# Fourth pair's loads behind a one-hot DMA, second pair's assignment in the PV bank, fourth pair's transposes later: the opening of a routed-attention and FFN kernel

## Chip, core and metric

The kernel runs on one core of one Trainium2 chip. The metric is the device time of one launch in microseconds (us). Before the change 12 runs gave a median of 343.56 us, from 342.28 to 346.72.

## What is computed

Attention with 4 batches, 8 heads, 768 positions and head size 64, in which a query sees only the keys that fall into its own one of 16 clusters, and then a gated feed-forward layer over all 3072 tokens:

```python
q_assign = argmax(einsum('bhsd,hcd->bhsc', q_n, c_n))      # k_assign likewise
scores   = where(q_assign == k_assign, q @ k.T / sqrt(64), -1e9)
attn     = softmax(scores) @ v                              # [4, 8, 768, 64]
x        = attn as [3072, 512]; xn = x / rms(x) * rms_g
out      = (silu(xn @ w_gate) * (xn @ w_val)) @ w_out       # 512 -> 1536 -> 512
```

## The kernel before, in words

**Work units.** Two heads of one batch are a pair; there are 16, numbered 0 to 15, so "the fourth pair" is pair 3. A head of a batch is a slot; pair p owns slots 2p and 2p+1. Each pair is prepared, then its two slots are scored, exponentiated and multiplied with v; the FFN of a batch follows while later slots are worked on.

**Preparing a pair** (`prep_parts`, L178 to L275) makes thirteen steps: four transpose groups T0 to T3 (L195: three 128x128 fp32 transposes on TensorE, then one copy of the 128x384 result out of PSUM, L199 or L201); CAST (L218) puts the transposed q and k as bf16 into `aug`; SP (L231) is the cluster product, eight small matmuls; TR, MX, CMP, SCL and BACK (L238 to L259) are the chain on VectorE that makes a one-hot row of it: transpose, maximum, compare, scale, transpose back into `ohT`; PLACE (L272) sends `ohT` by four DMAs of 24 KB into the lower rows of `aug`, one for each of two heads `a` and two sides (q or k); CASTV (L223) casts v on GpSimd. The mask is in the product itself: 64 rows of q or k and 16 rows of one-hot.

**The main loop** (L540 to L554) has 9 steps for a slot. At every third step `score_chunk` (L281) makes four matmuls into a PSUM tile of three banks (`scw`, two such tiles) and one exponential over 1536 columns on ScalarE (L302). I call these groups G0, G1, G2 (slot 0), G3 to G5 (slot 1) and so on, and their exponentials E0, E1 and so on. At steps 2 to 7 of a slot `pv_group` (L306) multiplies the slot before with v, in the one bank `acc`; at step 8 `pv_norm` (L316) divides by the sum on VectorE (L322, L323), and the next slot's product with v needs that bank back. From step 96 on the scores come in single chunks and each step also carries one piece of the FFN: gp, vp (L401) or dp (L434).

**What orders the work.** Nothing is scheduled: the order is written out by hand, and each engine takes its instructions in program order. `at(step, ...)` (L466) hangs a preparation step behind a loop step. All loads of q, k and v are on the queue of SyncE (SP), with three buffers for each of `q_in`, `k_in` and `v_in`: a fourth load waits until the first buffer's readers are done. Before the loop the PSUM tiles come from six banks `f`; from the loop on every transpose group and every cluster product takes the single bank `t` of `ps_t` (`t_tile`, L172), so each must wait until VectorE has read the one before it. Dummy matmuls (`keep_warm`, L125) fill TensorE before the loop.

**The opening** (L470 to L505). Pair 0 is prepared at once, pairs 1 and 2 are transposed, and so is group T0 of pair 3, into a tile that `keep_warm` has used (`late[3, 0]`, L484, L190). Then the loop starts with G0, which needs pair 0's one-hot rows. Pair 1's assignment hangs on steps 0 to 3, pair 2's on steps 4 to 18, pair 3's T1 to T3 on steps 10 to 15.

**The last batch.** Its rows are normalised after the loop by the plan of L513 to L521: `sumsq`, `inv`, `norm` (L367), and then a transposing DMA into `xnT` (L370), which the FFN of that half waits for.

Of the kernel before, what the change touches and what calls it, by code (L numbers as in the profile page):

```python
# [8 lines left out]
F32 = mybir.dt.float32  # L9
# [10 lines left out]
def kernel(  # L20
# [12 lines left out]
    nc = tc.nc  # L33
# [3 lines left out]
    P = 128  # L37
# [41 lines left out]
    def load_part(pi, kind, eng=nc.sync):  # L79
        b, hp = divmod(pi, NP)  # L80
        src, nm = ((q, "q_in"), (k, "k_in"), (v, "v_in"))[kind]
        src = src[b, 2 * hp:2 * hp + 2]
        tl = ld.tile([P, 2, ST * D], F32, name=nm, tag=nm)
        eng.dma_start(out=tl, in_=src.rearrange("h (p t) d -> p h (t d)", p=P))
        loads[pi, kind] = tl
# [5 lines left out]
    c_in = const.tile([P, D + 1], F32, name="c_in")  # L91
    nc.vector.memset(c_in[:, D:D + 1], 1e-15)
    nc.scalar.dma_start(out=c_in[:, 0:D], in_=centroids.rearrange("h c d -> (h c) d"))
    for pi in range(4):
        load_pair(pi, (0, 1))
    load_part(0, 2)
    g_b = const.tile([P, DM], F32, name="g_b")


# [78 lines left out]
    def prep_parts(pi):  # L178
        st = pi % NSET
        qk32 = [None]  # L180
        state = {}

        def t_group(g):
            a, side = divmod(g, 2)
            if qk32[0] is None:
                qk32[0] = prep.tile([P, 4, HS], F32, name="qk32", tag="qk32", bufs=3)
            if pi == 2 and g > 1:
                tp = ((ps_t, ps_pv)[g - 2]).tile([P, HS], F32, name="tp", tag=("t", "acc")[g - 2])
            elif (pi, g) in late:
                tp = late[pi, g][:, 0:HS]  # L190
            else:
                tp = t_tile("tp")
            src = loads[pi, side]
            for i in range(TH):
                nc.tensor.transpose(tp[:, i * P:(i + 1) * P], src[:, a, i * P:(i + 1) * P], ident_f)  # L195
            dst = qk32[0][:, g, :]
            on_dve = (g in (0, 3) if pi == 0 else g == 3 if pi == 2 else pi < 7 or g % 2)
            if on_dve:
                nc.vector.tensor_copy(dst, tp)  # L199
            else:  # L200
                nc.scalar.copy(dst, tp)  # L201
            state[g] = tp

        def casts():
            if pi == 0:
                for g in (0, 2, 1, 3):
                    a, side = divmod(g, 2)
                    for par in range(2):
                        dst = aug[0][a][0:D, side, par * HS:(par + 1) * HS]
                        src = state[g][par * D:(par + 1) * D, :]  # L210
                        if g == 3:
                            nc.vector.tensor_copy(dst, src)
                        else:
                            nc.scalar.copy(dst, src)
                return
            for a in range(2):
                for par in range(2):
                    nc.gpsimd.tensor_copy(aug[st][a][0:D, :, par * HS:(par + 1) * HS],  # L218
                                          qk32[0][par * D:(par + 1) * D, 2 * a:2 * a + 2, :])

        def casts_v():
            v_in = loads[pi, 2]
            nc.gpsimd.tensor_copy(vbf[st][:, :, :, 0:D],  # L223
                                  v_in[:, :, :].rearrange("p a (t d) -> p a t d", d=D))

        def assign():
            h0 = 2 * (pi % NP)
            sp = t_tile("sp")
            for j in range(4):
                side, a = divmod(j, 2)  # L230
                nc.tensor.matmul(sp[32 * j:32 * j + 32, :], lhsT=cbd[:, h0 + a, :, :].rearrange("p c r -> p (c r)"),  # L231
                                 rhs=qk32[0][:, 2 * a + side, :], start=True, stop=True,
                                 tile_position=(0, 32 * j))
            state["sp"] = sp

        def oh_tr():
            tr = prep.tile([P, HS], F32, name="tr", tag="tr")
            nc.vector.transpose(tr, state["sp"])  # L238
            state["tr"] = tr[:, :].rearrange("p (n c r) -> p n r c", c=NC, r=2)

        def oh_max():
            mx = small.tile([P, TH * 4, 2], F32, name="mx", tag="mx")
            nc.vector.tensor_reduce(mx, state["tr"], axis=AX, op=ALU.max)
            state["mx"] = mx

        def oh_cmp():
            oh = prep.tile([P, HS], BF16, name="oh", tag="oh")
            nc.vector.tensor_tensor(oh[:, :].rearrange("p (n c r) -> p n r c", c=NC, r=2), state["tr"],  # L248
                                    state["mx"].unsqueeze(3).to_broadcast([P, TH * 4, 2, NC]), op=ALU.is_ge)
            state["oh"] = oh  # L250

        def oh_scale():
            oh = state["oh"]
            nc.vector.tensor_scalar(oh[0:64, :], oh[0:64, :], scalar1=1.0, scalar2=MASK,
                                    op0=ALU.subtract, op1=ALU.mult)

        def oh_back():
            ohT = prep.tile([P, HS], BF16, name="ohT", tag="ohT")
            nc.vector.transpose(ohT, state["oh"])  # L259
            state["ohT"] = ohT  # L260

        def place():
            ohT = state["ohT"]
            for a in range(2):
                for side in range(2):
                    r = 32 * (2 * side + a)
                    eng = nc.sync
                    if pi == 0:
                        eng = nc.gpsimd if side else nc.scalar
                    elif pi == 1 and (a or side):  # L270
                        eng = nc.gpsimd
                    eng.dma_start(out=aug[st][a][D:KA, side, :].rearrange("c (r n) -> c r n", r=2),  # L272
                                  in_=ohT[r:r + 2 * NC, :])

        return [lambda: t_group(0), lambda: t_group(1), lambda: t_group(2), lambda: t_group(3), casts, assign, oh_tr, oh_max, oh_cmp, oh_scale, oh_back, place, casts_v]  # L275


# [188 lines left out]
    def at(step, fn):  # L466
        extra.setdefault(step, []).append(fn)
# [13 lines left out]
        p0[i]()  # L481
    for i in (T0, T1, T2, T3):
        p1[i]()
    late[3, 0] = keep_warm(3)  # L484
    for i in (T0, T2, T1, T3):
        p2[i]()
    p3[T0]()
    load_part(1, 2, nc.scalar)
    p1[CAST]()
    keep_warm(4)  # L490
    first.close()
    late["wide"] = wide.enter_context(tc.tile_pool(name="ps_wide", bufs=2, space=PSUM,
                                                 reuse_waits="tile"))
    at(2, p0[CASTV])
    for i, step in ((SP, 0), (TR, 0), (MX, 1), (CMP, 2), (SCL, 2), (BACK, 3), (PLACE, 3), (CASTV, 5)):
        at(step, p1[i])
    for i, step in ((T1, 10), (T2, 12), (T3, 15), (SP, 19), (TR, 20), (MX, 21), (CMP, 22), (SCL, 23), (BACK, 24),
                    (PLACE, 24), (CAST, 24), (CASTV, 28)):
        at(step, p3[i])
    for i, step in ((SP, 4), (TR, 5), (MX, 10), (CMP, 12), (SCL, 15), (BACK, 18), (PLACE, 18), (CAST, 6), (CASTV, 14)):  # L500
        at(step, p2[i])
    for pi in range(2, 4):
        at(3, lambda pi=pi: load_part(pi, 2))
# [5 lines left out]
    for b in range(B):  # L509
        sumsq, inv, norm, turn = rms_parts(b)  # L510
        if b == 0:
            plan = [(sumsq, (-9, -7, -4), (0, 1, 2), 0), (sumsq, (8, 8, 8), (0, 1, 2), 1), (inv, (8,), (0,), 2),
                    (norm, (12, 17, 18), (0, 1, 2)), (turn, (17, 20, 22), (0, 1, 2)),  # L513
                    (sumsq, (27, 29, 30), (3, 4, 5)), (inv, (30,), (1,)), (norm, (32, 33, 34), (3, 4, 5))]
        else:
            early = (8, 8, 9, 9, 10, 11, 12) if b == B - 1 else (9, 9, 10, 11, 12, 13, 15)
            plan = [(sumsq, early[:3], (0, 1, 2)), (inv, early[3:4], (0,)), (norm, early[4:], (0, 1, 2)),
                    (sumsq, (19, 19, 25), (3, 4, 5)), (inv, (26,), (1,)), (norm, (27, 28, 29), (3, 4, 5))]
        for fn, steps, items, *more in plan:
            for step, it in zip(steps, items):  # L520
                at(H * NCH * (b + 1) + step, lambda fn=fn, it=it, more=more: fn(it, *more))  # L521
    at(30, lambda: load_pair(6))
    for pi in range(4, B * NP):
        base = 2 * NCH * (pi - 2) + {7: 14, 8: 10, 9: 4}.get(pi, 0)
        steps = (-11, -8, -5, -2, 0, 0, 2, 3, 4, 5, 6, 7, 10)
        if pi == 6:
            steps = (-11, -8, -5, -2, 0, 0, 2, 3, 4, 4, 5, 6, 7)
        elif pi > 6:
            steps = (-8, -6, -4, -2, 0, 0, 2, 3, 4, 5, 6, 6, 10)
        for fn, step in zip(prep_parts(pi), steps):  # L530
            at(base + step, fn)
        if pi < B * NP - 3:
            at({6: 100, 7: 118}.get(pi, base + 12), lambda pi=pi: load_pair(pi + 3))
# [62 lines left out]
```

The softmax here doesn't subtract the row's maximum and nothing guards it: scores larger than these inputs give would overflow.

## Time and profile before

| what | value |
|---|---|
| median of 12 runs | 343.56 us |
| the profiled execution: time | 344.23 us |
| the profiled execution: span from first to last instruction | 342.4 us |
| mean granted TensorE clock | 1.000 |
| TensorE busy | 331.6 us, 97% of the span |
| VectorE busy | 222.7 us, 65% |
| ScalarE busy | 225.5 us, 66% |
| GpSimd busy | 89.0 us, 26% |
| DMA, mean over the span | 102 GB/s |

The span is cut by the profile into instructions with start and duration; the time of a run also holds 1.83 us around the span. The shares of busy time hide that the limits change: the opening (until G0 starts at 14.97 us), the loop without the FFN (until about 62 us), the loop with it (until about 267 us) and the FFN alone. The chain of waits is read from the end backwards: each piece is the work that released the next one.

### The profile page before, as it was taken

The numbers are of one execution on the slowest core, as the hardware profiler recorded it, in microseconds if no ns is written. First come the engines' busy times: TensorE is split into PE (matmuls) and PEld (weight loads), VectorE is DVE, ScalarE is ACT, GpSimd is POOL, SyncE is SP. The second block draws the span as 40 slices with busy tenths as digits, with TensorE's granted clock in tenths as the row PEclk, the third lists the DMA queues.
The fourth block names the chain that finished last, engine by engine and source line by source line (L and its number), as shares of the span: only waits on it lengthen the run. The fifth ranks groups of instructions, "written<-read, shape, count | busy, mean of one in ns | idle before, by whom it ended". The sixth has DMA issues, their size and how long they took to land.

```text
span 342.4 us, 7497 instructions
## 1 busy us (share of the span) xinstructions
PE 331.6 (97%) x2922; PEld 203.2 (59%) x2955; DVE 222.7 (65%) x460; ACT 225.5 (66%) x388; POOL 89.0 (26%) x123
## 2 busy tenths in 40 slices
PE   8899999999999999999999999999999999999996
PEld 4556666666666565666656566566666655555553
DVE  4787697698764777866475567774554687655540
ACT  4498999978776687766767677777777353323322
POOL 2577695066431133230111205010000011000000
PEclk9999999999999999999999999999999999999999
DMA  7747999909744125161501003120000022300012
GB/s 232 243 153 227 239 260 257 255 11 176 208 149 134 48 77 154 42 186 39 173 3 42 33 12 79 35 55 33 31 12 24 31 57 55 78 31 31 33 62 92
DMA packets 36771, 34.99 MB, mean 102 GB/s; under 512 B 13520, under 2 KB 33664, under 8 KB 36736
## 3 DMA queue, kind: packets, MB, share of 16 engines
q1 hardware_dynamic: 30240, 29.20, 27.7%
q0 software_dynamic: 5984, 4.84, 9.0%
q10 hardware_dynamic: 512, 0.48, 0.5%
q8 instruction: 23, 0.38, 0.5%
q14 instruction: 12, 0.10, 0.1%
HBM read 28.61 MB, written 6.29 MB: 102 GB/s over the span
## 4 chain that ended last, share of the span: by engine, by line
PE 86%; DVE 6%; ACT 3%; DMA 3%; issue 2%; POOLq 0%; POOL 0%; DVEq 0%; ACTq 0%
PE gp L401 17%; PE vp L401 17%; PE dp L434 17%; PE sc L299 12%; PE acc L313 9%; PE tp L195 5%; PE scw L299 3%; PE sp L231 3%; ACT pT L302 2%; DMA aug<-ohT 1%; PE w_ps L129 1%; DMA xnT<-xn 1%; DVE oh L248 1%; DVE tr L238 1%; DVE qk L199 1%
## 5 line engine op out<-in xcount | busy, mean ns | idle before, releaser
L302 ACT ACTIVATE pT<-sc 128x512 bf16<-128x512 f32 x192 | 113.8, 598 | 45.4 <-PE sc L299 44.9
L410 DVE SCALAR_TENSOR_TENSOR uu<-th,gp 128x384 f32<-128x384 f32 x96 | 53.0, 552 | 66.2 <-ACT th L406 66.1
L401 PE MATMUL gp<-xnT,wg 128*128 128x384 bf16 x384 | 78.1, 325 | 0.2
L401 PE MATMUL vp<-xnT,wv 128*128 128x384 bf16 x384 | 78.1, 325 | 0.2 <-DVE gvT L416 0.2
L406 ACT ACTIVATE th<-gp 128x384 f32<-128x384 f32 x96 | 47.3, 492 | 43.1 <-PE gp L401 40.5
L313 PEld LDWEIGHTS <-pT 128*128 128x128 bf16 x1152 | 57.1, 97 | 29.3 <-DVE x L323 2.6
L299 PE MATMUL sc<-aug 80*128 80x512 bf16 (+1 forms) x256 | 72.9, 326 | 0.0
L434 PE MATMUL dp<-wo,gvT 128*128 128x512 bf16 (+1 forms) x268 | 71.2, 369 | 1.6
L218 POOL CAST aug<-qk 64x768 bf16<-64x768 f32 x60 | 51.9, 866 | 52.6 <-DVE qk L199 34.4
L313 PE MATMUL acc<-vbf,pT 128*128 128x65 bf16 x1152 | 63.2, 194 | 1.4 <-DVE x L323 0.7
L416 DVE TENSOR_TENSOR gvT<-uu,vp 128x384 bf16<-128x384 f32 x96 | 52.6, 548 | 5.9 <-PE vp L401 0.8
L401 PEld LDWEIGHTS <-wg 128*128 128x128 bf16 x384 | 37.2, 97 | 30.4 <-issue 1.0
L401 PEld LDWEIGHTS <-wv 128*128 128x128 bf16 x384 | 37.1, 97 | 18.7 <-issue 0.6
L302 ACT ACTIVATE pT<-scw 128x1536 bf16<-128x1536 f32 x32 | 44.9, 1457 | 5.0 <-PE scw L299 4.5
L299 PEld LDWEIGHTS <-aug 80*128 80x128 bf16 x384 | 33.0, 97 | 18.1 <-issue 7.4
L434 PEld LDWEIGHTS <-gvT 128*128 128x128 bf16 x300 | 29.1, 98 | 24.4
L199 DVE COPY qk<-tp 128x384 f32<-128x384 f32 x40 | 21.8, 552 | 15.3 <-PE tp L195 15.0
L299 PE MATMUL scw<-aug 80*128 80x512 bf16 (+1 forms) x128 | 26.0, 325 | 1.1 <-DMA aug<-ohT 0.9
L358 POOL TENSOR_SCALAR ir<-ss 128x3 f32<-128x3 f32 x7 | 1.7, 237 | 95.2 <-ACT jk L344 83.4
L367 DVE SCALAR_TENSOR_TENSOR xn<-x,ir,g_b 128x512 bf16<-128x512 bf16 x24 | 20.3, 862 | 6.5 <-POOL ir L359 5.4
L223 POOL CAST vbf<-v_in 128x768 bf16<-128x768 f32 x16 | 13.4, 836 | 34.7 <-issue 34.3
L323 DVE TENSOR_TENSOR x<-acc,inv 128x384 bf16<-128x384 f32 x32 | 17.8, 557 | 1.1
(65 smaller groups left out, 210.0 us busy)
## 6 DMA issues: line engine op xcount, KB each, us to landing
q_in<-in_q_dram SPq DMA_DIRECT2D x16, 384.0 KB, 5.1
k_in<-in_k_dram SPq DMA_DIRECT2D x16, 384.0 KB, 5.8
out_dram<-ob SPq DMA_DIRECT2D x23, 256.0 KB, 2.0
v_in<-in_v_dram SPq DMA_DIRECT2D x15, 384.0 KB, 5.5
wg<-in_moe_w_gate_dram POOLq DMA_DIRECT2D x4, 384.0 KB, 10.7
wv<-in_moe_w_val_dram POOLq DMA_DIRECT2D x4, 384.0 KB, 11.3
wo<-in_moe_w_out_dram POOLq DMA_DIRECT2D x4, 384.0 KB, 7.0
aug<-ohT SPq DMA_DIRECT2D x57, 24.0 KB, 1.9
```

The source lines that it names most:

```text
L199: nc.vector.tensor_copy(dst, tp)
L218: nc.gpsimd.tensor_copy(aug[st][a][0:D, :, par * HS:(par + 1) * HS], qk32[0][par * D:(par + 1) * D, 2 * a:2 * a + 2, :])
L299: nc.tensor.matmul(sc[:, o:o + n], lhsT=ag[:, 1, kc * P:(kc + 1) * P], rhs=ag[:, 0, qo:qo + n], start=True, stop=True)
L302: nc.scalar.activation(pts[slot][:, j * CH:(j + nch) * CH], sc[:, :nch * CH], ACT.Exp, scale=scale)
L313: nc.tensor.matmul(acc[:, TORD[g], :], lhsT=pts[slot][:, kc * S + g * P:kc * S + (g + 1) * P], rhs=vb[:, a, TORD[kc], :], start=(kc == 0), ...
L323: nc.vector.tensor_tensor(x_t[b][:, :, h * D:(h + 1) * D], acc[:, :, 0:D], inv.to_broadcast([P, ST, D]), op=ALU.mult)
L367: nc.vector.scalar_tensor_tensor(st["xn"][:, tl, :], x_t[b][:, t, :], st["ir", m][:, tl:tl + 1], g_b, op0=ALU.mult, op1=ALU.mult)
L401: nc.tensor.matmul(pt[:, :HS], lhsT=w[:, dc, fc * P:(fc + 1) * P], rhs=xnT[b, m][:, :, dc, :], start=(dc == 0), stop=(dc == DC - 1))
L406: nc.scalar.activation(th, pt[:, :HS], ACT.Tanh, scale=0.5)
L410: nc.vector.scalar_tensor_tensor(uu, th, 1.0, pt[:, :HS], op0=ALU.add, op1=ALU.mult)
L416: nc.vector.tensor_tensor(gvT[half][:, fc, :], uu, pt[:, :HS], op=ALU.mult)
L434: nc.tensor.matmul(dp, lhsT=gvT[hf][:, f, tl * P:(tl + 1) * P], rhs=wo[:, f, cols], start=(f == 0), stop=(f == FC - 1))
```

## The change

- Loads: before the loop's order is laid down only q and k of pairs 0, 1 and 2 are asked for. q and k of pair 3 and v of pairs 0 and 1 are asked for later in the program, so that on SP's queue they stand behind one of pair 0's four one-hot DMAs, which moves from ScalarE's queue to SP's. v of pair 1 moves from ScalarE's queue to SP's.
- Pair 3's T0 moves from before G0 to step 5; T1, T2 and T3 from steps 10, 12 and 15 to 7, 9 and 11. It now uses bank `t`. One more dummy matmul stands before G0.
- Pair 1's cluster product goes to the bank `acc`; its CMP, SCL, BACK and PLACE move by one or two steps.
- Pair 2's SP to PLACE move from steps 4 to 18 to steps 13 to 19; pair 3's from 19 to 24 to 20 to 25. Pair 4's T0 and T1 stand one step later.
- In the last batch the second and third `norm` stand one step earlier.

```diff
-    for pi in range(4):
+    for pi in range(3):
         load_pair(pi, (0, 1))
-    load_part(0, 2)
...
-            elif (pi, g) in late:
-                tp = late[pi, g][:, 0:HS]
...
-            sp = t_tile("sp")
+            if pi == 1:
+                sp = ps_pv.tile([P, HS], F32, name="sp", tag="acc")
+            else:
+                sp = t_tile("sp")
...
-                    if pi == 0:
+                    if pi == 0 and (side or not a):
                         eng = nc.gpsimd if side else nc.scalar
...
-    late[3, 0] = keep_warm(3)
+    load_pair(3, (0, 1))
+    load_part(0, 2)
+    load_part(1, 2)
+    w_ps = keep_warm(3)
     for i in (T0, T2, T1, T3):
         p2[i]()
-    p3[T0]()
-    load_part(1, 2, nc.scalar)
     p1[CAST]()
-    keep_warm(4)
+    keep_warm(5, w_ps)
...
-    for i, step in ((SP, 0), (TR, 0), (MX, 1), (CMP, 2), (SCL, 2), (BACK, 3), (PLACE, 3), (CASTV, 5)):
+    for i, step in ((T0, 5), (T1, 7), (T2, 9), (T3, 11), (SP, 20), (TR, 21), (MX, 22), (CMP, 23), (SCL, 24), (BACK, 25),
+                    (PLACE, 25), (CAST, 25), (CASTV, 28)):
+        at(step, p3[i])
+    for i, step in ((SP, 0), (TR, 0), (MX, 1), (CMP, 3), (SCL, 4), (BACK, 5), (PLACE, 5), (CASTV, 5)):
         at(step, p1[i])
-    for i, step in ((T1, 10), (T2, 12), (T3, 15), (SP, 19), (TR, 20), (MX, 21), (CMP, 22), (SCL, 23), (BACK, 24),
-                    (PLACE, 24), (CAST, 24), (CASTV, 28)):
-        at(step, p3[i])
-    for i, step in ((SP, 4), (TR, 5), (MX, 10), (CMP, 12), (SCL, 15), (BACK, 18), (PLACE, 18), (CAST, 6), (CASTV, 14)):
+    for i, step in ((SP, 13), (TR, 14), (MX, 15), (CMP, 16), (SCL, 18), (BACK, 19), (PLACE, 19), (CAST, 6), (CASTV, 14)):
         at(step, p2[i])
...
-            early = (8, 8, 9, 9, 10, 11, 12) if b == B - 1 else (9, 9, 10, 11, 12, 13, 15)
+            early = (8, 8, 9, 9, 10, 10, 11) if b == B - 1 else (9, 9, 10, 11, 12, 13, 15)
...
-        if pi == 6:
+        if pi == 4:
+            steps = (-10, -7, -5, -2, 0, 0, 2, 3, 4, 5, 6, 7, 10)
+        elif pi == 6:
```

## The prediction, as put on record before the run

> **What bounds the kernel now.** I read the chain of waits first, because TensorE is 97% busy and a share that high says nothing about where a change can help. G0, E0 and so on are the score groups and exponentials as named above; T3.0 to T3.3 are pair 3's transpose groups.
>
> Chain of waits, in order of time (start us, length us, what):
>
> ```profile
> 11.83 3.09 DMA aug<-ohT
> 14.97 0.82 PE scw L299 x4
> ...
> 34.23 0.85 PE sp L231 x8
> ...
> 57.03 3.92 ACT pT L302 x3
> ...
> 278.65 0.81 PE vp L401 x4
> 280.34 3.74 DMA xnT<-xn
> 284.13 0.82 PE gp L401 x4
> ```
>
> The loop's start hangs on pair 0's one-hot DMA. From there to 30 us VectorE and TensorE take turns in the chain, to 54 us TensorE with the waits for `pv_norm`, then ScalarE, then TensorE. At 284.13 the transposed `xnT` of the last batch ends a wait. So only two places of the change touch the chain: the opening, and the `norm` steps.
>
> The table of stretches (length, then busy PE, PEld, DVE, ACT, POOL, granted clock, DMA share, GB/s) shows how tight the opening is:
>
> ```profile
> 20.00:25.00 5.00, 5.00 (x65) 3.31 (x64) 3.80 (x8) 5.00 (x5) 4.82 (x8) 1.00 0.68 211
> 25.00:30.00 5.00, 4.04 (x58) 2.84 (x54) 4.83 (x10) 4.18 (x4) 4.76 (x6) 1.00 0.77 231
> ```
>
> TensorE is full from 20 to 25, VectorE from 25 to 30: work moved into either stretch is paid there. The timeline (start, length, engine, idle time before) gives the durations:
>
> ```profile
> 11.56 1.31 ACTq L272 DMA_DIRECT2D aug<-ohT  x2
> 11.83 1.29 POOL L272 DMA_DIRECT2D aug<-ohT  x2 [7.20 <-DVE ohT L259]
> ...
> 15.72 0.85 PE L231 MATMUL sp<-qk,cbd 128*32 128x384 f32 x8
> ...
> 16.64 0.58 DVE L238 STREAM_TRANSPOSE tr<-sp 128x384 f32<-128x384 f32 x1 [2.36 <-PE sp L231]
> ...
> 18.76 0.58 DVE L259 STREAM_TRANSPOSE ohT<-oh 128x384 bf16<-128x384 bf16 x1
> ...
> 20.51 0.81 PE L299 MATMUL scw<-aug 80*128 80x512 bf16 x4
> ...
> 24.97 0.56 DVE L323 TENSOR_TENSOR x<-acc,inv 128x384 bf16<-128x384 f32 x1
> ...
> 25.78 0.81 PE L299 MATMUL scw<-aug 80*128 80x512 bf16 x4
> ```
>
> Seen from G0's start s = 14.97, VectorE begins pair 1's chain at s+1.67 and reaches BACK at s+3.79; G4 starts at 20.51, G7 at 25.78 behind the norm of slot 0.
>
> **One-hot of pair 0: -0.7 us.** G0 reads the two DMAs of head 0, which stay on ScalarE and GpSimd and are issued at the same time (11.56, 11.83); only one of head 1 moves to SP. The gain must come from the emptier queue: in the trace q and k of pair 3 and v of pair 0, issued at 6.01, 7.20 and 7.62, land at 12.4, 13.4 and 14.5. Pair 1's four one-hots, with little else in flight, took 2.1 to 2.7 us, median 2.4, against 3.09. So 11.83 + 2.4 = 14.23 for 14.92: G0 at 14.25, gain 0.7. Bounds: nothing, and 11.83 + 2.1 = 13.93, a gain of 1.0. TensorE is not later: T3.0 goes (0.36), one dummy matmul comes (0.21, from 1.03 less 0.17 over about four).
>
> [...]
>
> **The loads, late: hidden.** SP issues its one-hot (0.69) at 11.6, then q3, k3, v0, v1, v2 at about half a microsecond each from 12.3. A load into an empty queue landed 3.5 us (v1 on ScalarE's queue) to 4.1 us (v2 at 20.11) after its issue, and the next ones follow by 1.0 (384 KB at 376 to 399 GB/s): q3 16.1, k3 17.1, v0 18.1, v1 19.2. T3.0 can run at 16.4, its copy not before 18.0 (below); v0's cast of 0.83 ends at 19.0, and the first product with v comes at 20.1. Cover about 1 us each. v3 waits for v0's cast; behind it on SP stand pair 1's one-hot (ready 19.1) and pair 4's loads, needed after 28. Behind the cast on GpSimd stand three one-hots of pair 1 (G6, 24.3) and pair 2's casts. If v0 came over 1 us later, this cover would go and each further microsecond would count fully.
>
> **G0 to G4: +1.5 us against s.** Every T3 group takes bank `t` and must wait for VectorE's copy of the group before. With s = 14.25: the cluster product at s+0.75, TR, MX, CMP and SCL as in the trace from s+1.67, and T3.0's copy (0.56) in BACK's old place, s+3.79 to s+4.35. T3.1 starts at s+4.4, and G3 stands behind it: s+4.75, E3 at s+5.6 (before: 20.28, s+5.31). BACK then fills VectorE until s+4.93, T3.1's copy until s+5.5; T3.2 at s+5.55 (result after 0.52), its copy s+6.1 to s+6.65, T3.3 at s+6.7, and G4 behind it at s+7.06 = 21.3. Before, G4 stood at s+5.54. Net with the one-hot: 21.3 - 20.51 = +0.8.
>
> **G4 to G7: +0.3 us.** Before, pair 2's cluster product (0.79) ran between G1 and G2, where TensorE waited for exponentials; now it stands between G4 and G5, where TensorE is full. From G4's start: 0.65 + two products with v (0.36), cluster product, result at +1.87; then TR, MX, CMP (0.62 each) stand ahead of the norm of slot 0 on VectorE (0.15 + 0.56): done at +4.5 to +4.75, the larger where CMP shares time with GpSimd's casts (0.81 instead of 0.58 at 22.38). Then one product with v (0.19) and pair 3's cluster product (0.79): G7 at +5.5 to +5.75. Before: 25.78 - 20.51 = 5.27. Net at G7: +1.0 to +1.3; I take +1.1.
>
> **G7 to the end of the loop: 0.** The same instructions in the same order, but for pair 4's T0 and T1 one step later: one wait for the norm shortens as another grows. Chain pieces follow each other without a wait on anything at a fixed time (loads and weights are early), so the delay is carried whole. If some wait had slack that the chain doesn't show, up to 0.5 of it could be lost there.
>
> **The last batch: +0.4 us.** VectorE's order here:
>
> ```profile
> 277.38 0.75 DVE L367 SCALAR_TENSOR_TENSOR xn<-x,ir,g_b 128x512 bf16<-128x512 bf16 x1 [1.35 <-POOL ir L359]
> 278.05 0.55 DVE L416 TENSOR_TENSOR gvT<-uu,vp 128x384 bf16<-128x384 f32 x1
> 278.51 1.41 DVE L367 SCALAR_TENSOR_TENSOR xn<-x,ir,g_b 128x512 bf16<-128x512 bf16 x2
> ```
>
> All wait for `ir`, so an earlier place gains nothing: the three norms and the product together still end at 279.92. But the second norm now stands ahead of gvT, which ends at 279.3 instead of 278.60, and vp at 278.65 started just behind it (it reuses the PSUM tile that gvT reads). TensorE slips by 0.70. It had 0.25 to 0.3 in hand before `xnT` at 284.13 (three dp matmuls from 283.19 end at 283.84), so 0.4 remains. Bounds: 0, if the tile is free sooner than I read it, and 0.7. SP now issues this transpose ahead of one output DMA; the output has three buffers and waits harmlessly.
>
> **Sum.** -0.7 + 1.5 + 0.3 + 0.4 = +1.5 us. Against the profiled execution, 344.23 + 1.5 = 345.7; that execution is 0.67 above the median, and against the median it is **345.1 us**, 0.4% slower. The unknowns together: one-hot ±0.3 to 0.7, the shared time with GpSimd ±0.3, the last batch ±0.4: 343.9 to 346.4.
>
> **Rivals.**
> - *The exponentials keep up* (faster): E7 waited 0.82 us and E10 0.56 for scores, both because VectorE was late with a norm. If pair 2's chain, now in one piece, frees VectorE sooner there, and the gaps at G3 and G4 are refilled, the change is -0.7 - 0.82 - 0.56 + 0.4 = -1.7: 341.9. It decides at E7 before 26.6. For it: ScalarE was busy 5.00 of 5 from 20 to 25. Against it: T3.1 behind the copy is an order that no timing removes. 13%.
> - *The delay is absorbed*: the opening's loss meets slack before 62 us and only the last batch pays, or both cancel: 343.6, from 343.1 to 344.0. Against it stands the unbroken chain. 15%.
> - *v0 is late* (slower by more): the loads need 1.5 us each, v0 lands after 19.5, GpSimd stands at its cast with pair 1's one-hots and pair 2's casts behind it, and the product with v starts after 20.7. Price: another 1 to 2 us, 346.6. For it: v0 is now third in a queue that starts at 12.3. 12%.
> - Forecast: 60%.
>
> A difference under 0.5% (1.7 us) is about what a measurement of this kernel can't tell from none. The forecast's own spread puts about 45% of it beyond that: slower 0.12 + 0.60 x 0.45 plus a little for the unexpected, 0.42; faster 0.13; same 0.45. The range takes in most of both outer rivals: 342.5 to 347.0.
>
> **What would show it.** Right: G0 at about 14.2, a wait of TensorE for VectorE's copy before T3.1 and T3.3, G4 near 21.3, G7 near 26.9, and at the end vp starting behind gvT with `xnT` no longer the last to arrive. Wrong: E3 to E6 without a gap, G7 before 26, TensorE waiting for `v_in` or `q_in`, or a shift that is gone by 62 us.

## The result and the profile after

The changed kernel takes 346.25 us (median of 11 runs, 345.63 to 347.35); the kernel before takes 343.71 (median of 47 runs). The ratio after to before is 1.0067, 95% interval 1.0044 to 1.0089: slower by 2.3 us by the ratio and 2.5 by the medians, against 1.5 forecast. The profiled execution of the changed kernel took 347.35 us, the longest of the 11; its span is 345.6 us, its mean granted clock 0.999. Shares of busy time hardly moved: TensorE 332.7 us (96%), VectorE 222.6, ScalarE 225.6, GpSimd 89.1.

The chain of waits of the changed kernel, in order of time (start us, length us, what):

```profile
12.46 2.64 DMA aug<-ohT
15.24 0.81 PE scw L299 x4
16.05 0.83 PE sp L231 x8
...
19.49 0.55 PE tp L192 x3
...
21.89 0.55 PE tp L192 x3
...
23.46 0.83 PE sp L231 x8
...
25.51 1.16 DVE oh L248
...
27.76 0.83 PE sp L231 x8
```

The one-hot of pair 0 still ends last before G0, but flies 2.64 us instead of 3.09. Between G0 and 28 us the chain runs, among others, through two of pair 3's transpose groups (19.49, 21.89; I call the groups turns from here on), the cluster products of pairs 1 to 3 (16.05, 23.46, 27.76) and a compare of VectorE (L248). At the end, `xnT` is gone from the chain. The waits of TensorE in the same profile (who waits, for what: us in total, times, longest):

```profile
PE tp L192 <- DVE qk L196: 2.0, 3, 0.9
PE acc L313 <- DVE x L323: 1.6, 2, 0.9
...
PE vp L401 <- DVE gvT L416: 0.8, 2, 0.7
```

and of the kernel before:

```profile
PE tp L195 <- DVE qk L199: 0.8, 3, 0.4
PE acc L313 <- DVE x L323: 0.7, 2, 0.5
```

The turns wait for VectorE's copies 2.0 us in all, where they waited 0.8; the product with v waits 1.6 for the norm (before: 0.7), vp 0.8 for gvT (before: 0.2). The timeline of the changed kernel shows where (start, length, engine, idle time before):

```profile
15.24 0.81 PE L299 MATMUL scw<-aug 80*128 80x512 bf16 x4 [0.36 <-DMA aug<-ohT]
...
19.49 0.55 PE L192 MATMUL tp<-ident_f,k_in 128*128 128x128 f32 x3 [0.92 <-DVE qk L196]
19.88 0.81 PE L299 MATMUL scw<-aug 80*128 80x512 bf16 x4
20.69 0.55 PE L192 MATMUL tp<-ident_f,q_in 128*128 128x128 f32 x3
...
21.89 0.55 PE L192 MATMUL tp<-ident_f,k_in 128*128 128x128 f32 x3 [0.47 <-DVE qk L196]
22.27 0.81 PE L299 MATMUL scw<-aug 80*128 80x512 bf16 x4
...
23.39 0.85 PE L231 MATMUL sp<-qk,cbd 128*32 128x384 f32 x8
...
25.51 1.16 DVE L248 TENSOR_TENSOR oh<-tr,mx 128x384 bf16<-128x384 f32 x1
...
26.78 0.56 DVE L323 TENSOR_TENSOR x<-acc,inv 128x384 bf16<-128x384 f32 x1
27.40 0.36 PE L313 MATMUL acc<-vbf,pT 128*128 128x65 bf16 x6 [0.90 <-DVE x L323]
...
28.47 0.82 PE L299 MATMUL scw<-aug 80*128 80x512 bf16 x4
```

G0 is at 15.24, G3 at 19.88, G4 at 22.27 and G7 at 28.47. T3.1 waits 0.92 for the copy of T3.0 and T3.3 0.47; G7 stands behind a product with v that waits 0.90 for the norm of slot 0, and on VectorE that norm stands behind pair 2's compare, which took 1.16 us. In the view of stretches (length, then busy PE, PEld, DVE, ACT, POOL, clock, DMA share, GB/s) the full engines of before are no longer full:

```profile
20.00:25.00 5.00, 4.54 (x51) 2.71 (x49) 2.33 (x5) 3.31 (x3) 4.88 (x8) 1.00 0.72 214
25.00:30.00 5.00, 3.95 (x55) 2.27 (x54) 4.33 (x9) 3.50 (x3) 4.71 (x6) 1.00 0.48 170
```

ScalarE has 3.31 and 3.50 us of work in them where it had 5.00 and 4.18. The granted clock is 1.00 in both.

**Stage by stage.** Durations of one execution hold its chances, so both kernels were profiled again (the last experiment below). Columns: end of pair 0's `ohT` on VectorE; from there to G0; then from group to group; and from G10 to the end of the span (us).

| kernel | ohT | to G0 | G0–G4 | G4–G7 | G7–G10 | G10–end |
|---|---|---|---|---|---|---|
| before, the profile shown | 11.53 | 3.44 | 5.54 | 5.27 | 4.70 | 311.97 |
| before, again | 11.98 | 2.86 | 5.52 | 4.67 | 4.67 | 311.89 |
| after, the profile shown | 12.43 | 2.81 | 7.03 | 6.20 | 4.88 | 312.22 |
| after, again | 11.91 | 2.80 | 7.04 | 5.63 | 4.88 | 312.24 |

From the second profile of before (343.37 us) to that of after (346.28) the time grows by 2.91: -0.13 up to G0, +1.52 from G0 to G4, +0.96 from G4 to G7, +0.21 from G7 to G10 and +0.35 behind G10.

### The profile page after: what moved, and what is told of

It is laid out like the page before. It is cut to its first block, busy times and chain, and to the rows that moved or that the text cites. A ratio compares the mean times of both kernels' runs of the same rounds, so it can differ in the third digit from the quotient of the medians.

```text
span 345.6 us, 7500 instructions
## 1 busy us (share of the span) xinstructions
PE 332.7 (96%) x2923; PEld 203.9 (59%) x2956; DVE 222.6 (64%) x460; ACT 225.6 (65%) x388; POOL 89.1 (26%) x123
## 4 chain that ended last, share of the span: by engine, by line
PE 84%; DVE 8%; ACT 3%; issue 2%; DMA 1%; POOL 1%; POOLq 0%; ACTq 0%
PE gp L401 17%; PE vp L401 17%; PE dp L434 16%; PE sc L299 12%; PE acc L313 8%; PE tp L192 6%; PE sp L231 4%; PE scw L299 3%; ACT pT L302 2%; DMA aug<-ohT 1%; PE w_ps L128 1%; DVE oh L248 1%; DVE tr L238 1%; DVE mx L243 1%; DVE x L323 1%
```

## The experiments

The theory: the turns in bank `t` and pair 2's late product cost about 2.5 us between G0 and G7, the two norms 0.4; the late loads cost nothing. Rivals: v of pair 0 arrives late and holds GpSimd, or GpSimd's casts hold VectorE. Ratios are to the kernel before, on the same chip.

**1. The norms of the last batch put back** (changed kernel with the old steps):

```diff
-            early = (8, 8, 9, 9, 10, 10, 11) if b == B - 1 else (9, 9, 10, 11, 12, 13, 15)
+            early = (8, 8, 9, 9, 10, 11, 12) if b == B - 1 else (9, 9, 10, 11, 12, 13, 15)
```

> The changed kernel with only the last batch's norm steps put back (10, 11, 12). My theory (the second norm stands ahead of gvT and holds vp up by 0.7 us, of which 0.4 reaches the end): vp is no longer held 0.7 us by gvT, the next half's first gp starts just behind the landing of xnT again, and the time is 0.4 us under the changed kernel, that is 2.1 us over the kernel before. Rival (the wait at vp is made up later): the time is that of the changed kernel within 0.2 us, 2.5 us over before.

345.82 us, ratio 1.0057 (1.0038 to 1.0076): 0.3 (by the ratios) to 0.43 (by the medians) less than the changed kernel, as forecast, though the intervals overlap. The mechanism is in the trace. VectorE and TensorE of the changed kernel:

```profile
280.15 1.42 DVE L367 SCALAR_TENSOR_TENSOR xn<-x,ir,g_b 128x512 bf16<-128x512 bf16 x2 [1.34 <-POOL ir L359]
281.48 0.55 DVE L416 TENSOR_TENSOR gvT<-uu,vp 128x384 bf16<-128x384 f32 x1
...
282.08 0.81 PE L401 MATMUL vp<-xnT,wv 128*128 128x384 bf16 x4 [0.69 <-DVE gvT L416]
```

and of this experiment:

```profile
278.95 0.75 DVE L367 SCALAR_TENSOR_TENSOR xn<-x,ir,g_b 128x512 bf16<-128x512 bf16 x1 [1.35 <-POOL ir L359]
279.62 0.55 DVE L416 TENSOR_TENSOR gvT<-uu,vp 128x384 bf16<-128x384 f32 x1
...
280.22 0.81 PE L401 MATMUL vp<-xnT,wv 128*128 128x384 bf16 x4
```

With one norm ahead of gvT instead of two, vp starts without a wait. From G10 to the end this execution takes 311.56 us. Over all profiles of the record, the seven with the new norm steps take 312.21 to 312.36 there, the six with the old ones 311.56 to 311.97: the new steps lose between 0.24 and 0.8.

**2. The late loads alone** (the kernel before, with k of pair 3 and v of pairs 0 and 1 asked for behind pair 0's one-hot on SP):

```diff
-    for pi in range(4):
+    for pi in range(3):
         load_pair(pi, (0, 1))
-    load_part(0, 2)
+    load_part(3, 0)
...
-                    if pi == 0:
+                    if pi == 0 and (side or not a):
...
+    load_part(3, 1)
+    load_part(0, 2)
+    load_part(1, 2)
...
-    load_part(1, 2, nc.scalar)
```

> The kernel before with only the loads of k of the fourth pair and of v of pairs 0 and 1 moved behind pair 0's one-hot on SP's queue (q of the fourth pair stays early, since T0 stays early); all steps, banks and the last batch as before. My theory (the emptier queue brings the one-hot 0.6 us sooner, and late loads cost nothing): G0 starts 3.44 - 0.6 = 2.8 us after ohT, and the time is 0.3 to 0.7 us under the kernel before. Rival (the late loads are themselves the cause of the loss: v0's cast on GpSimd pushes pair 1's one-hots and pair 2's casts back): the time is 0.5 to 1.5 us over before.

343.40 us, ratio 0.9989 (0.9971 to 1.0007). From `ohT` to G0 it takes 2.87 us, and G4–G7 4.67 as in the second profile of before; G0–G4 is longer by 0.37 (5.89), where T3.1 waits 0.62 for pair 2's TR. Loads and one-hot together lie between a gain of 1.0 us and a loss of 0.2, so the changed kernel's loss of 2.5 comes from the rest of the change: the order of the steps and their banks.

**3. T1 to T3 of pair 3 at their old steps** (T0 stays in the loop):

```diff
-    for i, step in ((T0, 5), (T1, 7), (T2, 9), (T3, 11), (SP, 20), (TR, 21), (MX, 22), (CMP, 23), (SCL, 24), (BACK, 25),
+    for i, step in ((T0, 5), (T1, 10), (T2, 12), (T3, 15), (SP, 20), (TR, 21), (MX, 22), (CMP, 23), (SCL, 24), (BACK, 25),
```

> The changed kernel with only T1, T2 and T3 of the fourth pair put back from steps 7, 9, 11 to 10, 12, 15 (T0 stays at 5, pair 2's assignment at 13). Theory of the early place (the loss from G0 to G4 comes only from the turns standing ahead of G3 and G4): G3 and G4 start 0.9 and 1.5 us sooner and the time falls by about 1 us or more. Theory of bank t (the four turns and pair 2's and pair 3's cluster products go through one bank, each for a matmul and a VectorE step, and pair 2's product and chain only come later still when the turns do): G4 is sooner by about 1.5, but pair 2's CMP and the norm of slot 0 later, G7 is not sooner, and the time is within 0.5 us of the changed kernel.

347.33 us, ratio 1.0096 (1.0062 to 1.0129): slower still. Both expectations missed the time; the stages came as the second one said. G0–G4 fell to 5.77, but G4–G7 grew to 8.63. The turns now stand on both sides of pair 2's product, in the one bank that all of them need: the product waits 0.46 us for a copy, the last turn comes behind the product and its TR, VectorE waits 0.87 for that turn, and MX, CMP and the norm of slot 0 stand behind the turn's copy. TensorE in this experiment:

```profile
25.48 0.81 PE L299 MATMUL scw<-aug 80*128 80x512 bf16 x4
27.82 0.51 PE L313 MATMUL acc<-vbf,pT 128*128 128x65 bf16 x6 [1.53 <-DVE x L323]
28.26 1.51 PE L231 MATMUL sp<-qk,cbd 128*32 128x384 f32 x8
29.70 1.46 PE L299 MATMUL scw<-aug 80*128 80x512 bf16 x4
```

Product and score group take 1.51 and 1.46 us where they took 0.85 and 0.82. The stretches before and after 27.85 say why (the third column from the right is the granted clock):

```profile
24.45:27.85 3.40, 1.87 (x23) 1.21 (x22) 2.46 (x7) 2.90 (x2) 3.22 (x5) 1.00 0.91 296
27.85:31.20 3.35, 3.35 (x23) 1.34 (x24) 1.95 (x5) 0.00 (x0) 3.17 (x4) 0.50 0.13 35
```

After a stretch with TensorE busy 1.87 of 3.40 us the clock fell to 0.50 for 3.35 us. Of the six runs, the three with a mean clock of 0.994 or 0.995 took 347.9 to 348.6 us, the three at 0.998 to 1.000 took 345.9 to 346.8, no more than the changed kernel (345.6 to 347.4). So the order as such only moves the wait from the turns to the norm; what makes it slower is the clock. That the longer wait costs the clock is likely, but not shown: a mean clock of 0.995 or less also came in 6 of the 72 runs of the kernel before that were taken beside the experiments, and in one of the 12 of experiment 4.

**4. T3.1 in the bank of the product with v** (changed kernel):

```diff
+            elif pi == 3 and g == 1:
+                tp = ps_pv.tile([P, HS], F32, name="tp", tag="acc")
```

> The changed kernel with one transpose group, T1 of the fourth pair, in bank acc instead of bank t, so that it doesn't wait for VectorE's copy of T0. My theory (G3 and G4 stand behind transposes that wait for bank t): TensorE's wait of 0.9 us before T1 goes, G3 starts about 0.9 us sooner after G0 and G4 about 0.5 sooner, and the time falls by 0.4 to 0.7 us against the changed kernel, to about 2.0 us over before. Rival (the loss is made between G4 and G7 by VectorE, wherever G4 stands): G4 is sooner, G7 is not, and the time stays 2.5 over before.

345.64 us, ratio 1.0053 (1.0030 to 1.0075), 0.5 to 0.6 below the changed kernel, with overlapping intervals. G0–G4 fell from 7.03 to 6.13: the wait for the copy before T3.1 is gone. But TensorE then waits for two things that the turn had covered:

```profile
19.69 0.34 PE L315 MATMUL acc<-vbf,pT 128*128 128x65 bf16 x6 [0.56 <-POOL vbf L222]
...
24.10 0.81 PE L301 MATMUL scw<-aug 80*128 80x512 bf16 x4 [0.60 <-DMA aug<-ohT]
```

The first is v of pair 0, cast late; the second, at G6, pair 1's one-hot, which GpSimd issues behind that cast.

**5. Pair 2's casts of q and k later** (steps 6 to 17): `(CAST, 6)` becomes `(CAST, 17)`, to keep GpSimd's casts away from pair 2's chain on VectorE.

> The changed kernel with pair 2's casts on GpSimd moved from step 6 to step 17, behind pair 2's CMP in the order of the program. Theory (the casts hold pair 2's CMP on VectorE in most executions): CMP of pair 2 takes 0.6 us in the profile, G7 starts 5.6 us after G4, and the median falls by 0.2 to 0.6 us against the changed kernel. Rival (the casts hit some other VectorE step instead, or CMP is held only now and then): the median stays within 0.2 us.

346.67 us, ratio 1.0071 (1.0046 to 1.0096). It tells nothing about the theory: GpSimd was behind anyway, and the casts began at 22.71, where they had begun at 22.75 and 22.41. They still ran beside pair 2's CMP, which took 0.59 all the same. G4–G7 was 5.63, as in the second profile of the changed kernel.

**6. v of pair 0 asked for first** (changed kernel; `load_part(0, 2)` moved up, ahead of the one-hot on SP):

> The changed kernel with the load of v of pair 0 put back ahead of the one-hot (right behind pair 2's q and k). My theory for the part of the loss between G4 and G7 that I had too small (GpSimd, held by v0's cast at 19.7, makes pair 2's casts 1 us later, and they hold pair 2's CMP for 1.16 instead of 0.59): GpSimd's casts of pair 2 end before that CMP, it takes about 0.6, G7 is 0.5 us sooner after G4, and the time falls by 0.3 to 0.6 us against the changed kernel; the one-hot may land 0.1 to 0.2 later. Rival (the late v is not the cause): CMP or SCL is held as long as before and the time stays within 0.2 us of the changed kernel.

346.46 us, ratio 1.0077 (1.0047 to 1.0107): no gain. GpSimd in this experiment:

```profile
17.41 0.83 POOL L221 CAST vbf<-v_in 128x768 bf16<-128x768 f32 x1
20.21 1.51 POOL L273 DMA_DIRECT2D aug<-ohT  x3 [1.97 <-DVE ohT L260]
...
22.48 3.49 POOL L216 CAST aug<-qk 64x768 bf16<-64x768 f32 x4
```

v's cast comes 2.3 us earlier than in the changed kernel (19.72), and GpSimd then waits 1.97 for pair 1's `ohT`: pair 2's casts start where they did. The rival of the late v is refuted as the cause of the loss; pair 2's CMP took long here too (0.91), and G4–G7 was 5.95.

**7. The fourth turn in the loop, nothing else** (the late loads with q of pair 3 too, in the kernel before; T0 to T3 at steps 9, 11, 13, 15 in bank `t`):

```diff
-    late[3, 0] = keep_warm(3)
+    load_pair(3, (0, 1))
...
-    for i, step in ((T1, 10), (T2, 12), (T3, 15), (SP, 19), (TR, 20), (MX, 21), (CMP, 22), (SCL, 23), (BACK, 24),
+    for i, step in ((T0, 9), (T1, 11), (T2, 13), (T3, 15), (SP, 19), (TR, 20), (MX, 21), (CMP, 22), (SCL, 23), (BACK, 24),
```

> e2_loads_alone with q of the fourth pair behind the one-hot too, and so T0 of the fourth pair in the loop, in bank t: T0 to T3 at steps 9, 11, 13, 15 (before: T0 ahead of the loop, T1 to T3 at 10, 12, 15); pair 2's assignment stays early, the last batch as before. Theory of the fourth turn (one more matmul group of 0.36 and one more VectorE copy of 0.56 inside the crowded stretch, nothing hidden): 0.5 to 1.0 us over e2_loads_alone, 0.3 to 0.7 over the kernel before. Theory of pair 2's place (the opening is lost because pair 2's product and chain stand late, T0 itself is free): within 0.2 us of e2_loads_alone, 0.2 under before.

344.09 us, ratio 1.0006 (0.9988 to 1.0023), 0.6 to 0.7 above the loads alone (0.9989), with overlapping intervals. G0–G4 is 6.53 and G4–G7 5.15, against 5.89 and 4.67 there. One more turn in the loop, with its load late, costs about that much in a better order; the four turns of the changed kernel, packed ahead of pair 2's product, cost more.

**8. Pair 2's product early, in `acc`** (changed kernel; product at step 4 and chain at 8, 10, 12, 15, 18 as about in the kernel before):

```diff
-            if pi == 1:
+            if pi in (1, 2):
...
-    for i, step in ((SP, 13), (TR, 14), (MX, 15), (CMP, 16), (SCL, 18), (BACK, 19), (PLACE, 19), (CAST, 6), (CASTV, 14)):
+    for i, step in ((SP, 4), (TR, 8), (MX, 10), (CMP, 12), (SCL, 15), (BACK, 18), (PLACE, 18), (CAST, 6), (CASTV, 14)):
```

> The changed kernel with pair 2's assignment put back to about its old steps (product at 4, then 8, 10, 12, 15, 18, 18 instead of 13 to 19), its product in bank acc like pair 1's, so that the fourth pair's turns keep bank t; all else as changed. Theory of pair 2's place (its product costs 0.8 on a full TensorE and its chain stands ahead of the norm of slot 0): G7 starts about 4.7 us after G4 instead of 5.6 to 6.2, and the time is 0.6 to 1.2 us under the changed kernel. Rival (only the turns in front of G3 and G4 count): the time stays within 0.3 us of the changed kernel, or is longer because VectorE now has pair 2's TR between the turns' copies.

345.81 us, ratio 1.0049 (1.0032 to 1.0067), 0.4 to 0.6 below the changed kernel, with overlapping intervals. G4–G7 is 4.77, as in the kernel before, against 5.63; 0.35 of the 0.86 goes again by G10 (5.23 against 4.88), where the next norm is late: TensorE in this experiment waits 1.07 for it.

```profile
26.28 0.85 PE L231 MATMUL sp<-qk,cbd 128*32 128x384 f32 x8
...
31.54 0.34 PE L313 MATMUL acc<-vbf,pT 128*128 128x65 bf16 x6 [1.07 <-DVE x L323]
```

**9. Three repairs together** (changed kernel with T3.1 in `acc`, v of pair 0 early, the old norms):

> The changed kernel with three things at once: T1 of the fourth pair in bank acc, v of pair 0 loaded ahead of the one-hot, and the norm steps put back. If the three losses add up (0.6 for the bank, 0.4 for the norms, and v0, which held the first product with v by 0.6 us in e4_turn_in_acc once G4 came sooner): 1.2 to 1.6 us under the changed kernel, 1.0 over before. If the bank and the v load only trade places: about 1.0 under the changed kernel, 1.5 over before. In neither case does it reach the kernel before, since pair 2's product still stands between G4 and G5.

345.31 us, ratio 1.0021 (0.9990 to 1.0051): 0.9 below the changed kernel by the medians, near the sum of experiments 1 and 4. G0–G4 is 6.14, no better than with the turn in `acc` alone, so the early v again gave nothing. What is left stands between G4 and G7: 6.06, with pair 2's product in it and a wait of TensorE for the norm of 1.06.

**10. The best that the experiments point to** (the kernel before with the late loads of 2, and in the last batch all three norms behind gvT):

```diff
-            early = (8, 8, 9, 9, 10, 11, 12) if b == B - 1 else (9, 9, 10, 11, 12, 13, 15)
+            early = (8, 8, 9, 9, 11, 11, 11) if b == B - 1 else (9, 9, 10, 11, 12, 13, 15)
```

> The kernel before with the loads of e2_loads_alone (k of the fourth pair, v of pairs 0 and 1 behind pair 0's one-hot) and the last batch's three norms all at step 11, one step after gvT's place, instead of 10, 11, 12. My theory of the last batch (VectorE waits for ir with gvT queued behind the first norm; gvT ahead of all three costs nothing): gvT runs about 2 us sooner, vp doesn't wait for it, the three norms end 0.4 to 0.5 us sooner and with them xnT; 0.4 us off e2_loads_alone, 0.6 to 0.7 under the kernel before. Rival (the order of norms and gvT is not what holds TensorE there): the time is that of e2_loads_alone, 0.25 under before.

343.12 us beside 343.86, ratio 0.9974 (0.9956 to 0.9991): the only version that is below the kernel before by more than its interval; against the loads alone the intervals overlap. VectorE and TensorE of it:

```profile
276.08 0.55 DVE L416 TENSOR_TENSOR gvT<-uu,vp 128x384 bf16<-128x384 f32 x1
277.32 2.08 DVE L367 SCALAR_TENSOR_TENSOR xn<-x,ir,g_b 128x512 bf16<-128x512 bf16 x3 [0.69 <-POOL ir L359]
...
278.40 0.81 PE L401 MATMUL vp<-xnT,wv 128*128 128x384 bf16 x4
```

In this profile pair 4's turns waited 0.8 and 0.5 for `q_in` and `k_in` (G7–G10 5.29), which the loads alone did not show (4.68): in some executions the late loads have a price there. gvT now fills VectorE's wait for `ir` instead of standing behind it. Counting from the gp that starts ahead of this place to the first gp of the new half, it takes 7.79 us (275.81 to 283.60), in the second profile of before 8.29 and of after 8.63. But the loads alone and experiment 1, with the old norms, take 7.98: there `xnT` was in time, while in both profiles of before SP issued it 0.4 us behind the last norm instead of 0.1, and it ended a wait. So 0.2 of the 0.5 is the order of the norms, the rest is that wait.

**11. Both kernels profiled again.**

> The kernel before once more, for a second profile: ohT of pair 0 between 11.0 and 12.4, G0 3.4 us behind it if the one-hot's delay by the loads is regular, G4 5.5 behind G0, G7 5.3 behind G4 or less where GpSimd holds less.

> The changed kernel once more, for a second profile: ohT of pair 0 ended 0.9 us later in its first profile than in that of the kernel before, at a place that the change doesn't touch. If that is chance, it ends between 11.2 and 12.0 here; if it belongs to the change, again near 12.4. G0 2.8 us behind it, G4 7.0 behind G0, G7 5.6 or 6.2 behind G4, by whether GpSimd holds pair 2's CMP.

343.37 and 346.28 us; the stages are in the table above. TensorE in the second profile of before:

```profile
14.84 0.81 PE L299 MATMUL scw<-aug 80*128 80x512 bf16 x4 [0.30 <-ACT qk L201]
...
20.36 0.81 PE L299 MATMUL scw<-aug 80*128 80x512 bf16 x4
...
25.03 0.81 PE L299 MATMUL scw<-aug 80*128 80x512 bf16 x4
```

G0 waits for a copy of ScalarE here, not for the one-hot. And VectorE of both profiles of before, at pair 2's SCL:

```profile
23.94 0.90 DVE L254 TENSOR_SCALAR oh<-oh 64x384 bf16<-64x384 bf16 x1
```

```profile
23.79 0.24 DVE L254 TENSOR_SCALAR oh<-oh 64x384 bf16<-64x384 bf16 x1
```

The norm of slot 0 stands behind it: in the first profile it held the product with v for 0.54 us, in the second not at all.

## Why the prediction was right or wrong

- **One-hot of pair 0: -0.7 us. Wrong in size.** After, G0 stands 2.80 us behind `ohT`, near the 2.7 forecast (14.25 less 11.53), in part by luck: the forecast let GpSimd's DMA land last, after 2.4 us; it took 2.2, and ScalarE's, issued 0.3 earlier, landed last after 2.64. Before, G0 stands at that place too: 2.86 in the second profile, and in the loads alone 2.87, both times waiting for a copy. The 3.44 of the first profile, from which the step was worked out, did not come again. The term is about -0.1, near the lower of its bounds, no gain; that the one-hot is regularly late behind the loads is not shown. In the first profile of before, where k of pair 3 and v of pair 0 landed at 13.4 and 14.5, the two one-hots of head 0 flew 3.2 and 3.09 us; in the second, with the same loads ahead of it, GpSimd's was issued at 12.29 and had landed when G0 started at 14.84, so it flew 2.55 at the most, where it had flown 3.09.
- **The loads, late: hidden. Right, but with less cover than stated.** v's cast started at 19.72, 4.5 us behind G0 (forecast 3.9), waiting for the load. The first product with v came 5.83 behind G0 all the same, since T3.2 stood ahead of it. Experiment 4 shows the cover gone: 0.56 of wait, and 0.60 more at G6 for pair 1's one-hots behind the cast (0.68 in experiment 8).
- **G0 to G4: +1.5 us against s. Right**: +1.52, with the waits before T3.1 and T3.3 that it named, and the turns and copies each within 0.15 us of the place it gave. Experiment 4 takes one of them away and gets 0.9 of it back up to G4.
- **G4 to G7: +0.3 us. Wrong in size, the largest error.** After, it takes 5.63 in the second profile and in experiments 1, 4 and 5, inside the 5.5 to 5.75 that the step worked out; in the first profile 6.20, since the compare took 1.16 us, longer than the 0.81 allowed for. The 5.27 of before, which was taken away from it, held a stall of VectorE (SCL at 23.94, 0.90 us) that the second profile does not have (at 23.79, 0.24 us); there it is 4.67, as in the loads alone and in experiment 10. So the term is +0.96. The mechanism was as stated: TensorE's work between the groups is the same within 0.1 (product of 0.79 in, two turns of 0.36 out), and the rest is the stand for the norm behind pair 2's TR, MX and CMP. Experiment 8 moves the product and chain away and gets 0.86 of it back.
- **G7 to the end of the loop: 0. Off by +0.2**: G7–G10 is 4.85 to 4.91 in the kernels that hold pair 4's T0 and T1 one step later (but for 5.23 in experiment 8), 4.67 to 4.70 with the old steps (but for 5.29 in experiment 10). The trace shows T1 behind the product that waits for the norm; this was not tried by itself. Behind G10 the delay is carried whole, as forecast.
- **The last batch: +0.4 us. Right**, with vp waiting 0.69 for gvT (0.70 forecast): +0.35 behind G10 between the second profiles, 0.3 to 0.43 in experiment 1. The time in hand before `xnT`, taken off in the forecast, holds for the two profiles of before alone; where `xnT` was in time, as in experiment 1, the whole delay counts (311.56 against 312.24).
- **Sum**: +1.5 forecast, +2.9 between the second profiles, +2.5 between the medians. Of the 1.4 between the first two, 0.6 is the one-hot, 0.66 G4–G7 and 0.2 pair 4. The two large ones are errors in what was taken away, stages of one profile of before, and not in the forecast of the changed kernel.
- **Rivals.** *Exponentials keep up* fell: no gap at G3 and G4 was refilled, ScalarE is emptier. *The delay is absorbed* fell: no slack behind G10. *v0 is late* had its first half (the late cast); its price shows only where the turns no longer cover it (experiments 4 and 8), and with v early again the time did not fall (experiment 6).

Left open: why `ohT` of pair 0 ends between 11.2 and 12.5 us in the span from execution to execution, in code that the change doesn't touch; it adds about 1 us of spread to each profiled time, in both kernels. What pair 1's product in `acc` does by itself was not tried either.

## What to carry to other kernels

Transposes or products that share one PSUM bank cost a copy's time each as soon as nothing else stands between them (T3.2 to T3.3 in the changed kernel: 1.20 us, of which TensorE works 0.36 on the turn and VectorE 0.56 on the copy): count every turn in such a bank as a round trip of two engines, and see what the next norm or product stands behind. Before a difference of half a microsecond is built on a stage of one profile, profile the kernel a second time: here three stages of the changed kernel were forecast within 0.1 us of its second profile (one of them about 0.5 below its first), and the base was off by 0.6 twice. An instruction whose input is late belongs behind one that is ready, where an engine takes its instructions in the order of the program: with gvT ahead of the three norms VectorE waited 0.69 us for `ir` and vp did not wait (experiment 10); with gvT behind two of them the waits were 1.34 and 0.69 (the changed kernel).

## What the runs showed of the hardware

- **TensorE's clock was halved after a stretch that was far from idle.** In experiment 3 the clock was 0.50 for 3.35 us after 3.40 us in which TensorE was busy for 1.87, with one wait of 1.53; waits of 0.63 to 1.07 for the norm left it at 1.00 in the other kernels, and so did one of 1.31 before G0 in experiment 7, whose mean clock was 1.000. In the changed kernel TensorE was busy for 2.04 us of the 3.40 from 18.60 to 22.00, and the clock was 1.00 there and in the 3.40 us behind. What the clock goes by is open.

- **Where pair 2's compare on VectorE ran beside GpSimd's casts, one of the two took longer, now the one, now the other.** The compare took 1.16 us in one execution of the changed kernel and 0.59 in another, with GpSimd's four casts beside it both times. GpSimd in the first and the second profile of the changed kernel:

```profile
22.75 3.48 POOL L215 CAST aug<-qk 64x768 bf16<-64x768 f32 x4
```

```profile
22.41 3.82 POOL L215 CAST aug<-qk 64x768 bf16<-64x768 f32 x4
```

Where the compare took 1.16 us, the casts took 3.48, near the 3.43 of pair 1's casts (14.02), beside which VectorE mostly waits; where it took 0.59, they took 3.82. It is not always one alone: in the first profile of before both took longer, with casts of 3.72 beside a CMP of 0.81 and an SCL of 0.90; in the second the casts took 3.82, the CMP 0.84 and the SCL 0.24. What decides which of the two takes longer is not shown: no run here steered it.
